# A convolution and SiLU MLP on one core: the first block's taps on square TensorE tiles, and one weight unit rounded in thirds

## The chip, the cores and the metric

The kernel runs on one core of one Trainium2 chip. Its time is the device time of one execution in microseconds (us); the median of several executions is what is compared. The core has five engines with their own instruction queues: TensorE (PE; its weight loads are shown as PEld), VectorE (DVE), ScalarE (ACT), GpSimd (POOL) and SyncE (SP, which here only issues DMAs). Every queue runs in order: an instruction that waits holds up all that stand behind it in its queue.

## The reference

Two stages, 32768 tokens (8 sequences of 4096), 192 channels:

```python
# 1. causal convolution over 7 positions, one softmaxed filter per head (8 heads of 24 channels)
w = softmax(weight)                                  # [8 heads, 7 taps]
out[b, s, h, g] = sum_k w[h, k] * x_pad[b, s + k, h, g]      # x_pad: 6 zeros ahead of each sequence
# 2. an MLP over the tokens, no biases
h = x @ w_in                                         # [32768,192] x [192,2048]
g = h * (1.0 / (1.0 + np.exp(-h)))                   # SiLU
return (g @ w_out).astype(np.float32)                # [32768,2048] x [2048,192]
```

`x` and `weight` are float32; `w_in` and `w_out` come as float64 and are turned into float32 on the chip by integer arithmetic on their two 32-bit words ("rounding" below).

## The kernel before, in words

**Tiling.** The tokens are worked off in 32 blocks of 1024. A block lies as two halves (n = 0, 1) of 512 tokens; its 192 channels lie as three thirds (k = 0, 1, 2) of 64 channels. In tile `xt` partitions 0 to 63 hold the channels of half 0 and partitions 64 to 127 the same channels of half 1, with six tokens of halo ahead of each. The 2048 hidden columns are four units (j = 0 to 3) of 512: a unit of `w_in` is `wr[j]`, a unit of `w_out` is `wo[j]`.

**Blocks 1 to 31** use a saving (Winograd-like) product scheme, `product` (L497) and `out_slot` (L570), whose order is written out by hand in `PLAN`. The change doesn't touch them. **Block 0** is done plainly while the weights are still being rounded, and it is all that the change touches.

**Block 0, in the order of the program.** Almost all instructions are pinned: each engine gets them in program order. `heat` gives TensorE dummy products until data is there. The softmaxed taps reach all partitions by one small product (L365). Then thirds 0 and 1 of the convolution are made on TensorE: `diagonal(k)` lets ScalarE write seven diagonal matrices (the taps of each channel, twice side by side in 128 columns), and `conv_pe(k)` multiplies them with seven shifted views of `xt` (L805, 28 products in all, 64 rows by 128 columns, one per tap, third and half). The two column halves are the same, so the result is already there twice, on partitions 0 to 63 and 64 to 127; ScalarE copies it (`act.copy`, 128x512) into `dups[0]`. Third 2 is convolved on VectorE: `conv(0, 2, i)` is one ScalarE operation for the first tap (L404) and six on VectorE (L409), and `spread` (L421) duplicates it by DMA.

**Rounding.** `round_in(j, k)` rounds one third of unit j (128x256 operations), `round_in(j)` a whole one (128x768). Each has seven or eight VectorE operations, and for units 0 and 1 two of the steps are ScalarE's (`act.sign` and an `act.activation`): VectorE must wait for them, and they stand in ScalarE's queue in program order. Unit 0 is rounded in thirds, units 1 to 3 whole.

**The first products.** `up_plain(0, j)` (L460) makes h of unit j: 24 products of 64 rows by 128 columns into eight PSUM banks (two halves a of the columns, two halves n of the tokens, two 128-column groups e), three thirds k accumulated in each. For unit 0 the thirds are the outer loop, so all eight banks are opened with third 0; for the others each pair of banks is finished before the next. After a bank's last third ScalarE reads it with SiLU. There are only eight PSUM buffers in the pool (`bank()`), handed out in turn, so `up_plain(0, 1)` gets a bank back when ScalarE has read it for unit 0, and two of the banks of unit 0 are those that hold convolved third 1 until it is copied out. ScalarE needs a table load between the functions of the rounding and SiLU.

After that come the other units of `up_plain`, `down_plain` (L599), and block 1. `load` (L128), `halo` (L146) and `load_in` (L218, L223) issue the DMAs for x, its halo and the raw words of `w_in`; the halos of thirds 1 and 2 are issued by GpSimd behind a VectorE memset.

Of the kernel before, what the change touches and what calls it, by code (L numbers as in the profile page):

```python
# [9 lines left out]
F32 = mybir.dt.float32  # L10
# [7 lines left out]
def kernel(  # L18
# [24 lines left out]
    nc = tc.nc  # L43
# [3 lines left out]
    H, K = weight.shape  # L47
    NT = B * S
    DFF = moe_w_in.shape[1]
    P = 128  # L50
    R = 64
    NK = D // R
    grp = D // H
    pad = K - 1
    TB = 512
# [4 lines left out]
    NJ = NM // 2  # L60
# [11 lines left out]
    gpool = ctx.enter_context(tc.tile_pool(name="gp", bufs=2 * NJ))  # L72
    upool = ctx.enter_context(tc.tile_pool(name="up", bufs=13))
# [29 lines left out]
    def pin(ins):  # L103
        return tc.keep_in_program_order(ins)
# [7 lines left out]

    vec, act = Pinned(nc.vector), Pinned(nc.scalar)

    def bank():
        return psum.tile([P, TB], F32, tag="ps", name="ps")

    nats, xts, gs = {}, {}, {}

    def load(b, ks=range(NK)):  # L120
        if b not in nats:
            nats[b] = xpool.tile([P, NK, TB // SQ, SQ], F32, tag="nat", name="nat")
        nat = nats[b]
        for k in ks:
            for i in range(P // SQ):
                c = R * k + SQ * (i % 2)
                queue = nc.scalar if not b and k == 0 and i % 2 == 0 else nc.sync
                ins = queue.dma_start(  # L128
                    out=nat[SQ * i : SQ * i + SQ, k, :, :],
                    in_=x_v[2 * b + i // 2][:, :, c : c + SQ],  # L130
                )
                if not b:
                    pin(ins)
# [10 lines left out]
    def halo(k, queue):  # L144
        pin(
            queue.dma_start(  # L146
                out=xts[0][R:P, k, 0:pad], in_=x0[:, k, :], allow_slow_non_contiguous=True
            )
        )

    halo(0, nc.sync)

    zeros = const.tile([P, P], F32, name="zeros")
    warm = const.tile([P, 1], F32, name="warm")
# [3 lines left out]

    hot = const.tile([KR, 2, R], F32, name="hot")
    wown = const.tile([KR, NK, K], F32, name="wown")  # L160
    one_hot = upool.tile([P, TB], F32, tag="u", name="one_hot")[:, 0:P]
    vec.memset(wown, 0.0)
    vec.memset(one_hot, 0.0)
    pool = Pinned(nc.gpsimd)
# [1 line left out]
    for k in range(NK):  # L166
        rows_k = hot[SQ * k : SQ * k + SQ]
        for sign, base in ((1, 0), (-1, grp - 1)):
# [6 lines left out]
                pattern=[[0, 2], [sign, R]],  # L175
# [1 line left out]
            )  # L177

    for e in range(2):
        half = one_hot[R * e : R * e + R].rearrange("p (a c) -> p a c", a=2)  # L180
        pool.affine_select(
            out=half,
            in_=half,
            compare_op=ALU.not_equal,
            fill=1.0,
            base=0,
            pattern=[[0, 2], [-1, R]],
            channel_multiplier=1,
        )
    pool.memset(xts[0][0:R, :, 0:pad], 0.0)  # L190
# [15 lines left out]
        return raws[key]  # L206


    AS = ["p (k a c) -> p a k c"] + ["p (a k c) -> p a k c"] * (NJ - 1)

    def load_in(j, queue, ks=None):

        if ("i", j) not in raws:
            raw_tile(("i", j))
        raw = raws["i", j].rearrange(AS[j], a=2, k=NK)
        for e in range(2) if ks is None else ():
            for a in range(2):
                queue.dma_start(  # L218
                    out=raw[R * e : R * e + R, a, :, :], in_=in32[:, :, a, 2 * j + e, :]
                )  # L220
        for k in ks or ():
            for e in range(2):
                queue.dma_start(  # L223
                    out=raw[R * e : R * e + R, :, k, :], in_=in32[:, k, :, 2 * j + e, :]
                )
# [53 lines left out]
    def round_in(j, k=None):  # L279

        words = raws["i", j].rearrange(AS[j], a=2, k=NK)
        words = words.rearrange("p a k (c t) -> p a k c t", t=2)
        if k is None:
            rounded(
                wr[j].rearrange("p a k c -> p a (k c)"),
                words.rearrange("p a k c t -> p a (k c) t"),
                j < 2,
            )
        else:
            rounded(wr[j][:, :, k, :], words[:, :, k], j < 2)  # L290
        if k in (None, NK - 1):

            del raws["i", j]
            for e in range(2):
                nc.gpsimd.dma_start(
                    out=ws[j][R * e : R * e + R], in_=wr[j][R - R * e : 2 * R - R * e]
                )
# [8 lines left out]
    def comb(out, u, v, op):  # L306
        nc.gpsimd.tensor_tensor(out, u, v, op=op)
# [13 lines left out]
    def combine_out(j):  # L321


        def a_(u, a):
            return wo[j][:, a, :, HD * u : HD * u + HD]
# [4 lines left out]
        comb(x_[2], a_(0, 1), x_[1], ALU.subtract)  # L330
        comb(a_(1, 0), a_(0, 0), a_(1, 0), ALU.subtract)

    load_in(0, nc.sync, (0,))


    def heat(times):
        for _ in range(times):
            pin(
                nc.tensor.matmul(  # L339
                    idle[:, 0 : 2 * P],  # L340
                    zeros,
                    zeros.unsqueeze(1).to_broadcast([P, 2, P]),
                    start=True,
                    stop=True,
                )
            )
# [5 lines left out]
    heat(4)  # L352
    vec.tensor_reduce(top, wexp, axis=AX.X, op=ALU.max, negate=True)
    act.activation(wexp, wexp, AF.Exp, bias=top, accum_out=total)
    load(0, (1, 2))
    load_in(0, nc.sync, (1, 2))
    vec.tensor_scalar(total, total, scalar1=1e-9, scalar2=None, op0=ALU.add)
    vec.reciprocal(part_, total)
# [11 lines left out]
            stop=True,  # L370
        )
    )
    heat(2)
    vec.tensor_copy(taps.rearrange("p k i -> p (k i)"), by_head)

    tails = {}
# [1 line left out]
    def turn_in(b, k):  # L378
        if k == 0 and b:
            xt = xts[b] = xpool.tile([P, NK, pad + TB], F32, tag="xt", name="xt")  # L380
            if b * TT % S == 0:
                nc.gpsimd.memset(xt[0:R, :, 0:pad], 0.0)
            else:
                nc.gpsimd.tensor_copy(xt[0:R, :, 0:pad], tails.pop(b))
        xt = xts[b]
        pin(
            nc.vector.transpose(
                xt[:, k, pad : pad + TB], nats[b][:, k, :, :].rearrange("p k c -> p (k c)")
            )
        )  # L390
        if k == NK - 1:
            if b:
                nc.sync.dma_start(out=xt[R:P, :, 0:pad], in_=xt[0:R, :, TB : TB + pad])
            if (b + 1) * TT % S:
                tails[b + 1] = xpool.tile([R, NK, pad], F32, tag="tail", name="tail", bufs=2)
                nc.sync.dma_start(out=tails[b + 1], in_=xt[R:P, :, TB : TB + pad])
# [28 lines left out]
    dups, wins = {}, {}  # L425
# [12 lines left out]
        )[i]  # L438
        pin(nc.vector.tensor_tensor(t[:, i, :], u, v, op=ALU.subtract))

    def rows(t, e):
        return t[R * e : R * e + R]

    def g_tile(b, j, a):
        if (b, j, a) not in gs:
            gs[b, j, a] = gpool.tile([P, 2, 2, TB], F32, tag="g", name="g")
# [2 lines left out]
    def up_plain(b, j):  # L449

        d = dups[b]
        outs = [(a, n) for a in range(2) for n in range(2)]
        hs = {(a, n, e): bank() for a, n in outs for e in range(2)}
        order = [(k, o) for k in range(NK) for o in outs]
        if j:
            order = [(k, o) for o in outs for k in range(NK)]
        for k, (a, n) in order:
            for e in range(2):
                pin(
                    nc.tensor.matmul(  # L460
                        hs[a, n, e],
                        rows(wr[j], e)[:, a, k, :],
                        rows(d, e)[:, n, k, :],
                        start=k == 0,
                        stop=k == NK - 1,
                    )
                )
            if k == NK - 1:
                for e in range(2):
                    g = g_tile(b, j, a)  # L470
                    act.activation(g[:, n, e, :], hs[a, n, e], AF.Silu)
# [317 lines left out]

    diag = gpool.tile([P, NK - 1, K, P], F32, tag="g", name="diag")
    dups[0] = xpool.tile([P, 2, NK, TB], F32, tag="dup", name="dup")
    by_pe = {}

    def diagonal(k):
        for i in range(K):
            act.activation(diag[:, k, i, :], one_hot, AF.Copy, scale=taps[:, k, i : i + 1])

    def conv_pe(k):  # L800
        by_pe[k] = [bank() for _ in range(2)]
        for i in range(K):
            for n in range(2):
                pin(
                    nc.tensor.matmul(  # L805
                        by_pe[k][n],
                        rows(diag, n)[:, k, i, :],
                        rows(xts[0], n)[:, k, i : i + TB],
                        start=i == 0,
                        stop=i == K - 1,  # L810
                    )
                )

    turn_in(0, 0)

    vec.memset(xts[0][R:P, 1:NK, 0:pad], 0.0)
    for k in range(1, NK):
        halo(k, nc.gpsimd)
    diagonal(0)
    conv_pe(0)  # L820
    round_in(0, 0)
    diagonal(1)
    turn_in(0, 1)
    conv_pe(1)
    for j in (1, 2):
        load_in(j, nc.sync)
    turn_in(0, 2)
    conv(0, 2, 0)
    for n in range(2):
        act.copy(dups[0][:, n, 0, :], by_pe[0][n])  # L830
    for i in range(1, K):
        conv(0, 2, i)
    spread(0, 2)
    load_in(3, nc.sync)
    round_in(0, 1)
    for n in range(2):
        act.copy(dups[0][:, n, 1, :], by_pe[1][n])
    round_in(0, 2)
    round_in(1)
    for j in range(NJ):  # L840
        up_plain(0, j)
        if j + 2 < NJ:
# [70 lines left out]
```

## Time and profile before

| what | value |
|---|---|
| median of 4 runs (lowest to highest) | 2409.33 us (2409.12 to 2409.73) |
| the profiled execution's own time, and its span | 2410.11 us, 2408.4 us |
| busy share of the span: PE, DVE, ACT | 100%, 86%, 41% |
| TensorE, taps of block 0 (L805) | 7.28 to 19.50 us |
| TensorE, four units of h (L460) | 19.50 to 60.70 us, 10.3 us each |
| TensorE, product with w_out (L599) | 60.70 to 102.05 us |

The span is counted from the first instruction that the profile shows; times "at 7.28 us" are from there. A product of float32 shows as two matmul records. An instruction's line is L111 when it was issued through the helper that pins it. In lines of a timeline the columns are start, time from the first start to the last end, engine, line, operation, output<-inputs, shape and count, and in brackets the idle time of that engine before it with what ended it.

### The profile page before, as it was taken

How to read it: one execution, taken by the hardware profiler on the slowest of the kernel's cores; microseconds unless marked ns; L12 is line 12 of the kernel's file. 1: busy time of each engine (PE TensorE's matmuls, PEld its weight loads, DVE VectorE, ACT ScalarE, POOL GpSimd, SP SyncE). 2: the span in 40 equal slices, each digit the busy share in tenths (PEclk: the TensorE clock that was granted, in tenths of full speed). 3: DMA queues.
4: the chain of work that ended last, by engine and by line, in shares of the span. 5: the costliest groups of instructions: out<-in, count | busy, mean ns of one | idle time of the engine just before them, and what ended most of it. 6: DMA issues, size and time to landing. Idle time of an engine off the chain costs nothing.

```text
span 2408.4 us, 43335 instructions
## 1 busy us (share of the span) xinstructions
PE 2400.7 (100%) x17878; PEld 943.3 (39%) x17878; DVE 2061.7 (86%) x2812; ACT 993.9 (41%) x1873; POOL 70.1 (3%) x99
## 2 busy tenths in 40 slices
PE   9999999999999999999999999999999999999998
PEld 4333443334433344333344333443334433334433
DVE  8789888888888898888988888888889888898876
ACT  4334543334533345433454333453334533345432
POOL 4300000000000000000000000000000000000000
PEclk9999999999999999999999999999999999999999
DMA  7322122221222222222222222122222222222220
GB/s 160 60 44 47 35 36 54 53 41 32 42 47 53 41 41 36 45 54 44 44 38 36 54 50 43 32 39 51 53 41 41 36 45 54 43 43 39 36 40 14
DMA packets 453718, 110.59 MB, mean 46 GB/s; under 512 B 424080, under 2 KB 429200, under 8 KB 453520
## 3 DMA queue, kind: packets, MB, share of 16 engines
q1 hardware_dynamic: 449872, 105.85, 23.9%
q8 instruction: 140, 2.29, 0.4%
q0 software_dynamic: 448, 1.58, 0.3%
q10 hardware_dynamic: 3200, 0.39, 0.1%
q14 instruction: 58, 0.48, 0.1%
HBM read 31.46 MB, written 25.17 MB: 24 GB/s over the span
## 4 chain that ended last, share of the span: by engine, by line
PE 100%; DVE 0%; ACT 0%; issue 0%; ACTq 0%
PE ps L497 49%; PE ps L570 47%; PE ps L599 2%; PE ps L460 2%; PE ps L805 1%; PE ps L339 0%; DVE cmb L111 0%; ACT u L111 0%; DVE osb L111 0%; PE ps L365 0%; ACTq L739 0%; DVE zeros L111 0%; DVE warm L111 0%; ACTq L111 0%
## 5 line engine op out<-in xcount | busy, mean ns | idle before, releaser
L497 PE MATMUL ps<-dup,ws 64*128 64x512 f32 x2480 | 870.0, 589 | 0.0
L570 PE MATMUL ps<-g,wo 128*32 128x512 f32 x2976 | 661.8, 593 | 0.0
L521 DVE TENSOR_TENSOR g<-u,ps 128x512 f32<-128x512 f32 x744 | 486.0, 681 | 119.2 <-PE ps L497 89.8
L497 PE MATMUL ps<-win,wr 64*128 64x512 f32 x1488 | 567.8, 589 | 0.0
L570 PE MATMUL ps<-t,wo 128*32 128x128 f32 (+2 forms) x4528 | 500.6, 446 | 0.0
L518 ACT ACTIVATE g<-g 128x512 f32<-128x512 f32 x744 | 444.6, 631 | 97.3 <-DVE g L521 97.3
L497 PEld LDWEIGHTS ps<-dup,ws 64*128 64x128 f32 x2480 | 363.4, 187 | 291.8 <-issue 277.7
L570 PE MATMUL ps<-t,wx 128*32 128x512 f32 x2976 | 452.8, 592 | 0.0
L409 DVE SCALAR_TENSOR_TENSOR nat<-xt,taps,nat 128x512 f32<-128x512 f32 x564 | 423.5, 751 | 18.3 <-ACT nat L404 3.7
L497 PE MATMUL ps<-dup,wr 64*128 64x512 f32 x992 | 420.1, 596 | 0.0
L512 ACT COPY u<-ps 128x512 f32<-128x512 f32 x496 | 277.7, 588 | 229.3 <-PE ps L497 226.2
L638 ACT COPY cmb<-ps 96x512 f32<-96x512 f32 x30 | 17.4, 581 | 805.3 <-PE ps L570 805.3
L538 DVE TENSOR_TENSOR t<-g 128x1024 f32<-128x1024 f32 x248 | 299.9, 1220 | 27.2 <-PE ps L570 27.2
L538 DVE TENSOR_TENSOR t<-g,t 128x1024 f32<-128x1024 f32 x248 | 303.2, 1223 | 13.6 <-PE ps L570 3.2
L497 PEld LDWEIGHTS ps<-win,wr 64*128 64x128 f32 x1488 | 233.6, 187 | 175.3 <-issue 147.0
L570 PEld LDWEIGHTS ps<-t,wo 128*32 128x32 f32 x4528 | 180.4, 110 | 219.7 <-issue 199.5
L497 PE MATMUL ps<-win,ws 64*128 64x512 f32 x496 | 242.2, 589 | 0.0
L570 PE MATMUL ps<-g,wx 128*32 128x512 f32 x1488 | 234.6, 592 | 0.0
L570 PEld LDWEIGHTS ps<-t,wx 128*32 128x32 f32 x2976 | 121.9, 110 | 278.8 <-issue 269.5
L650 DVE TENSOR_TENSOR cmb<-cmb,ps 96x512 f32<-96x512 f32 x150 | 102.2, 681 | 135.2 <-ACT u L635 133.1
L497 PEld LDWEIGHTS ps<-dup,wr 64*128 64x128 f32 x992 | 160.6, 187 | 128.1 <-issue 114.2
L570 PEld LDWEIGHTS ps<-g,wo 128*32 128x32 f32 x2976 | 168.6, 110 | 98.3 <-issue 98.3
(72 smaller groups left out, 1224.9 us busy)
## 6 DMA issues: line engine op xcount, KB each, us to landing
dup<-nat SPq DMA_DIRECT2D x376, 128.0 KB, 2.3
nat<-in_x_dram SPq DMA_DIRECT2D x382, 64.0 KB, 2.4
out_dram<-osb SPq DMA_DIRECT2D x376, 64.0 KB, 2.0
raw<-in_moe_w_out_dram SPq DMA_DIRECT2D x8, 384.0 KB, 4.0
raw<-in_moe_w_in_dram SPq DMA_DIRECT2D x12, 192.0 KB, 4.5
ws<-wr POOLq DMA_DIRECT2D x8, 192.0 KB, 4.3
raw<-in_moe_w_in_dram SPq DMA_DIRECT2D x6, 128.0 KB, 3.0
xt<-xt SPq DMA_DIRECT2D x31, 4.5 KB, 1.9
```

Of the source, the lines that this page charges most:

```text
L409: nc.vector.scalar_tensor_tensor(out=dst, in0=src, scalar=tap, in1=dst, op0=ALU.mult, op1=ALU.add)
L460: nc.tensor.matmul(hs[a, n, e], rows(wr[j], e)[:, a, k, :], rows(d, e)[:, n, k, :], start=k == 0, stop=k == NK - 1,)
L497: nc.tensor.matmul(bk[b, m, bn], rows(w, half), rows(v, half), start=first, stop=True, skip_group_check=True,)
L512: pin(copy(u, bk[b, m, "1"]))
L518: pin(nc.scalar.activation(g, g, AF.Silu))
L521: pin(nc.vector.tensor_tensor(g, us.pop((b, m, i)), bk[b, m, bn], op=ALU.add))
L538: pin(nc.vector.tensor_tensor(t[i // 2][:, i % 2, :], u, v, op=ALU.subtract))
L570: nc.tensor.matmul(accs[b][at][SQ * q : SQ * q + SQ, to], lhs[:, e, SQ * k : SQ * k + SQ], rhs[:, e, ts(q, TB // 4) if i == 5 else to], st ...
L599: nc.tensor.matmul(acc[k][R * n : R * n + R, :], wo[j][:, a, e, R * k : R * k + R], gs[b, j, a][:, n, e, :], start=j == 0 and a == 0 and e ...
L638: pin(nc.scalar.copy(c[0], acc[0][0:n, :]))
L650: pin(nc.vector.tensor_tensor(out_, u, v, op=ALU.add))
L805: nc.tensor.matmul(by_pe[k][n], rows(diag, n)[:, k, i, :], rows(xts[0], n)[:, k, i : i + TB], start=i == 0, stop=i == K - 1,)
```

## The change

Six edits, all in block 0:

- The diagonal matrices have 64 columns in place of 128, so a tap product writes 64 PSUM partitions. Third k writes partitions 64k to 64k+63 of the bank of its token half: rows come from half n, columns from third k. For each tap the four products (two halves, two thirds) stand next to each other in the queue; all taps of both thirds are one loop (28 products as before).
- The result is there only once, so each is copied twice: `from_pe(k)` issues four 64x512 ScalarE copies per third, eight in all in place of four 128x512.
- Third 1 of `xt` is transposed ahead of the rounding of unit 0's first third, and its four loads are issued ahead of the halo of third 0 and of the first raw words of `w_in`.
- Five dummy products stand behind the tap matrix in place of two.
- Unit 1 of `w_in` is rounded by thirds: 3 x 8 operations of 128x256, with six ScalarE steps in place of two. Its raw words are laid out by thirds for that (`AS`).
- `up_plain(0, 1)` takes thirds as its outer loop, as unit 0 does.

```diff
-    halo(0, nc.sync)
-    one_hot = upool.tile([P, TB], F32, tag="u", name="one_hot")[:, 0:P]
+    one_hot = upool.tile([P, TB], F32, tag="u", name="one_hot")[:, 0:R]
...
-    AS = ["p (k a c) -> p a k c"] + ["p (a k c) -> p a k c"] * (NJ - 1)
+    AS = ["p (k a c) -> p a k c"] * 2 + ["p (a k c) -> p a k c"] * (NJ - 2)
...
+    load(0, (1,))
+    halo(0, nc.sync)
     load_in(0, nc.sync, (0,))
...
-    load(0, (1, 2))
+    load(0, (2,))
     load_in(0, nc.sync, (1, 2))
...
-    heat(2)
+    heat(5)
...
-        if j:
+        if j > 1:
             order = [(k, o) for o in outs for k in range(NK)]
...
-    diag = gpool.tile([P, NK - 1, K, P], F32, tag="g", name="diag")
+    diag = gpool.tile([P, NK - 1, K, R], F32, tag="g", name="diag")
     dups[0] = xpool.tile([P, 2, NK, TB], F32, tag="dup", name="dup")
-    by_pe = {}
-    def diagonal(k): ...
-    def conv_pe(k): ...
+    by_pe = [bank() for _ in range(2)]
     turn_in(0, 0)
     vec.memset(xts[0][R:P, 1:NK, 0:pad], 0.0)
     for k in range(1, NK):
         halo(k, nc.gpsimd)
-    diagonal(0)
-    conv_pe(0)
+    for i in range(K):
+        for k in range(NK - 1):
+            act.activation(diag[:, k, i, :], one_hot, AF.Copy, scale=taps[:, k, i : i + 1])
+    turn_in(0, 1)
+    for i in range(K):
+        for n in range(2):
+            for k in range(NK - 1):
+                pin(
+                    nc.tensor.matmul(
+                        by_pe[n][R * k : R * k + R, :],
+                        rows(diag, n)[:, k, i, :],
+                        rows(xts[0], n)[:, k, i : i + TB],
+                        start=i == 0,
+                        stop=i == K - 1,
+                    )
+                )
     round_in(0, 0)
-    diagonal(1)
-    turn_in(0, 1)
-    conv_pe(1)
     for j in (1, 2):
         load_in(j, nc.sync)
     turn_in(0, 2)
     conv(0, 2, 0)
-    for n in range(2):
-        act.copy(dups[0][:, n, 0, :], by_pe[0][n])
+    def from_pe(k):
+        for n in range(2):
+            for e in range(2):
+                act.copy(rows(dups[0], e)[:, n, k, :], by_pe[n][R * k : R * k + R, :])
+    from_pe(0)
     for i in range(1, K):
         conv(0, 2, i)
     spread(0, 2)
     load_in(3, nc.sync)
     round_in(0, 1)
-    for n in range(2):
-        act.copy(dups[0][:, n, 1, :], by_pe[1][n])
+    from_pe(1)
     round_in(0, 2)
-    round_in(1)
+    for k in range(NK):
+        round_in(1, k)
     for j in range(NJ):
         up_plain(0, j)
```

More of the change, by code (lines that the diff above doesn't have):

```diff
@@ L113, with rows @@
     vec, act = Pinned(nc.vector), Pinned(nc.scalar)
+    def rows(t, e):
+        return t[R * e : R * e + R]
     def bank():
@@ L179 @@
     for e in range(2):
-        half = one_hot[R * e : R * e + R].rearrange("p (a c) -> p a c", a=2)
+        half = rows(one_hot, e)
         pool.affine_select(
@@ L186 @@
             base=0,
-            pattern=[[0, 2], [-1, R]],
+            pattern=[[-1, R]],
             channel_multiplier=1,
@@ L439, in win @@
         pin(nc.vector.tensor_tensor(t[:, i, :], u, v, op=ALU.subtract))
-    def rows(t, e):
-        return t[R * e : R * e + R]
     def g_tile(b, j, a):
@@ L788, in finish @@
             store(2, cols)
-    diag = gpool.tile([P, NK - 1, K, P], F32, tag="g", name="diag")
+    diag = gpool.tile([P, NK - 1, K, R], F32, tag="g", name="diag")
     dups[0] = xpool.tile([P, 2, NK, TB], F32, tag="dup", name="dup")
-    by_pe = {}
-    def diagonal(k):
-        for i in range(K):
+    by_pe = [bank() for _ in range(2)]
+    turn_in(0, 0)
+    vec.memset(xts[0][R:P, 1:NK, 0:pad], 0.0)
+    for k in range(1, NK):
+        halo(k, nc.gpsimd)
+    for i in range(K):
+        for k in range(NK - 1):
             act.activation(diag[:, k, i, :], one_hot, AF.Copy, scale=taps[:, k, i : i + 1])
-    def conv_pe(k):
-        by_pe[k] = [bank() for _ in range(2)]
-        for i in range(K):
-            for n in range(2):
+    turn_in(0, 1)
+    for i in range(K):
+        for n in range(2):
+            for k in range(NK - 1):
                 pin(
                     nc.tensor.matmul(
-                        by_pe[k][n],
+                        by_pe[n][R * k : R * k + R, :],
                         rows(diag, n)[:, k, i, :],
@@ L812, in conv_pe @@
                 )
[L814 to L818, printed above, removed]
-    diagonal(0)
-    conv_pe(0)
     round_in(0, 0)
-    diagonal(1)
-    turn_in(0, 1)
-    conv_pe(1)
     for j in (1, 2):
@@ L835 @@
     round_in(0, 1)
-    for n in range(2):
-        act.copy(dups[0][:, n, 1, :], by_pe[1][n])
+    from_pe(1)
     round_in(0, 2)
-    round_in(1)
+    for k in range(NK):
+        round_in(1, k)
     for j in range(NJ):
```

## The prediction, made before the changed kernel was run

> **What bounds the kernel now.** First the page's busy times and its chain of work that ended last, then that chain in order of time for the first 110 us.
>
> ```profile
> span 2408.4 us, 43335 instructions
> ...
> PE 100%; DVE 0%; ACT 0%; issue 0%; ACTq 0%
> ```
> ```profile
> 1.14 3.78 PE ps L339 x8
> ...
> 7.28 12.22 PE ps L805 x56
> 19.50 41.20 PE ps L460 x192
> 60.70 41.35 PE ps L599 x192
> ```
>
> TensorE works without a gap from 1.14 us to its last product. The change touches nothing behind the first four units of h, so its worth is one number: how much earlier or later TensorE reaches the third unit (j=2), now at 19.34 + 2 x 10.3 = 39.9 us. Everything behind moves by that, unless something else is late there. So the second thing to read is what feeds TensorE before that: VectorE's and ScalarE's timelines.
>
> ```profile
> 7.14 0.61 DVE L111 TENSOR_SCALAR two<-raw 128x256 int32<-128x256 int32 x2 [0.67 <-DMA raw<-in_moe_w_in_dram]
> ...
> 11.10 0.71 DVE L387 STREAM_TRANSPOSE xt<-nat 128x512 f32<-128x512 f32 x1 [0.55 <-DMA nat<-in_x_dram]
> 12.65 4.69 DVE L409 SCALAR_TENSOR_TENSOR nat<-xt,taps,nat 128x512 f32<-128x512 f32 x6 [0.84 <-ACT nat L404]
> 17.26 0.49 DVE L111 TENSOR_SCALAR two<-raw 128x256 int32<-128x256 int32 x2
> ...
> 19.95 0.50 DVE L111 TENSOR_SCALAR two<-raw 128x256 int32<-128x256 int32 x2
> ...
> 22.55 1.02 DVE L111 TENSOR_SCALAR two<-raw 128x768 int32<-128x768 int32 x2
> ...
> 28.25 1.04 DVE L111 TENSOR_SCALAR two<-raw 128x768 int32<-128x768 int32 x2
> ```
> ```profile
> 17.78 0.72 ACT L111 ACTIVATE two<-two 128x256 int32<-128x256 int32 x2 [3.18 <-DVE two L111]
> 19.54 1.07 ACT L111 COPY dup<-ps 128x512 f32<-128x512 f32 x2 [1.03 <-PE ps L805]
> ...
> 23.61 1.58 ACT L111 ACTIVATE two<-two 128x768 int32<-128x768 int32 x2 [2.38 <-DVE two L111]
> 25.20 1.28 ACT L111 ACT_TABLE_LOAD   x1
> 27.26 4.03 ACT L111 ACTIVATE g<-ps 128x512 f32<-128x512 f32 x8 [0.77 <-PE ps L460]
> ```
>
> VectorE is full from 12.65 us on: six convolution steps, then rounding, a third of a unit in 2.65 us (17.26, 19.95, 22.55), unit 1 whole in 5.70. ScalarE's last rounding step is over at 25.19, the table is loaded by 26.48, and the first SiLU starts at 27.26, when TensorE has a bank ready: 0.8 us to spare. That is the tightest place, and the change adds work ahead of it on both engines.
>
> **Part by part.**
>
> *Square tiles.* 28 tap products now take 0.43 us each, two row tiles side by side. Four column tiles already run side by side in the later blocks: four records start within 0.02 us and the next four 0.43 us later.
>
> ```profile
> 600.12 0.61 PE L570 MATMUL ps<-t,wx 128*32 128x512 f32 x3
> 600.13 0.59 PE L570 MATMUL ps<-t,wo 128*32 128x512 f32 x1
> ```
>
> Two rows by two columns is not in this trace; the bounds are 7 x 0.86 = 6.0 us (four at a time) and 28 x 0.43 = 12.0 us (two at a time). I take 6.0, as both directions are seen to run in parallel, and leave 12.0 to a rival.
>
> *When the taps can start.* The fourth product needs the halo of third 1, which until now had until 13.4 us. GpSimd issues it at 6.77 us behind VectorE's memset and it lands 3.1 us later, at 9.9. Memset and issue stay where they are. The five dummy products end between 8.3 and 9.5 us (0.85 us each from 5.24, or half of that from 7.2 us on, where the tap products show the double rate), so they are covered by that wait; if the halo came at once they would cost about 1.1 us against the old start. Taps: 9.9 to 16.1 us with 0.2 us for start and drain, 3.4 us earlier than 19.50. Fourteen 64-column diagonals in place of fourteen of 128 take at most the old 0.30 us each and are there by 9.9; the wait for the halo covers them.
>
> *Copies.* Four in place of two per third: 0.59 + 3 x 0.48 = 2.05 us (a 32x512 copy of the later blocks takes 579 ns, so fewer partitions buy nothing). TensorE could start on h after the first, at 16.8 us, and needs all four for third 0 by 18.2.
>
> The row is 1.07 us for two copies. [...]
>
> *The loads.* SP issues eight loads of x in 4.30 us, 0.54 each. Four of them now pass the first raw words: 4 x 0.44 to 0.54 = 1.7 to 2.2 us, so the first rounding starts at 8.9 to 9.3 in place of 7.14, or less if the transfers overtake; not below 7.14. I take 8.8. Rounding 2.70 us to 11.5, transpose of third 2 (0.71, now behind it alone, its loads having kept their place in the queue and their old arrival at 11.1) to 12.2, ScalarE's first tap 0.84 to 13.05, six steps 4.61: VectorE is free at 17.7 in place of 17.26 (17.2 to 18.2). The earlier transpose of third 1 costs nothing, it falls into the wait for the raw words.
>
> *ScalarE's order.* Behind the first four copies (18.2) stands the pair of rounding steps of third 1 (17.7 + 0.53 = 18.2; 0.72 us), and only behind that the copies of third 1: 18.95 to 21.0. They also free the last two of unit 0's eight banks. So TensorE's last product of third 0 waits until 21.1, and nine products of that row tile follow at 0.86: unit 0 is done at 28.8 in place of 29.6. Of the 3.4 us, 0.8 are left.
>
> *Unit 1 in thirds.* 3 x 2.65 = 7.95 us for 5.70. Its last third starts on VectorE at 17.7 + 2.69 + 2.60 + 2 x 2.65 = 28.3; add 0.2 for waits on ScalarE behind the copies: 28.5. Its ScalarE pair, +0.53 and 0.72: 29.75; table load 1.28: 31.0; only then the first SiLU, 0.62: TensorE gets its first bank for unit 1 at 31.7. It has stood still since 28.8, 2.9 us. Unit 1 with thirds outermost needs all eight banks at once, and they come 0.49 us apart (4.03 us for eight): the last at 35.1. Nine products of 0.86 follow: unit 2 starts at 42.8 in place of 39.9. **Sum: +2.9 us.**
>
> *Behind it.* Rounding of unit 1 ends at 28.5 + 2.65 = 31.15 in place of 28.25, +2.9 too, so VectorE and GpSimd keep their distance to TensorE; unit 2's weights, done at 35.35, had 4.6 us to spare. No new wait there.
>
> **The rivals.**
>
> (1) *Slower, the tiles run two at a time.* Then the taps end at 22.1, the copies at 24.2, and ScalarE's pair for third 1 starts at 24.2 in place of 18.2: all rounding is 6 us later and the sum is +8.9 us: 2418.2. Against it are the four parallel column tiles above. It decides from a tap end of 16.2 us on: each us beyond it is a us on VectorE, so a late halo counts the same way.
>
> (2) *Not slower: ScalarE is free in time.* Were the SiLUs not held up, TensorE could go on at 28.8, but unit 2's weights come 7.1 us (28.25 to 35.35) after unit 1's at 31.15, at 38.3: at best 1.6 us faster, 2407.7. For it: VectorE may get through earlier. Against: with the third-2 loads at their old place it can't be free before 17.26, which leaves +2.4 us, and the order of the SiLUs behind unit 1's last third is fixed.
>
> (3) *The clock falls in the stall.* In the trace it does so at the end: the last product ends at 2401.8, and the clock is halved only at 2406.71, behind a stretch of 3.4 us with nothing on TensorE.
>
> ```profile
> 2399.89:2403.30 3.41, 1.94 (x40) 0.94 (x32) 2.19 (x7) 1.42 (x6) 0.00 (x0) 1.00 0.56 90
> 2403.30:2406.71 3.41, 0.00 (x0) 0.00 (x0) 1.09 (x3) 0.33 (x1) 0.00 (x0) 1.00 0.52 87
> 2406.71:2408.40 1.69, 0.00 (x0) 0.00 (x0) 0.00 (x0) 0.00 (x0) 0.00 (x0) 0.50 0.02 5
> ```
>
> (Columns: stretch, length, busy time of PE, PEld, DVE, ACT and POOL, clock, DMA share, GB/s.) A stall of 2.9 us is under 3.4. Should it fall, the start of the kernel shows the way back: 6 us from the first product to the double rate, up to 3.0 us lost: 2415.2.
>
> [...]
>
> **How the numbers follow.** The profiled execution took 2410.11 (span 2408.4 and 1.7 around it), 0.78 above the median, so: span 2411.3, that execution 2413.0, median 2409.33 + 2.9 = **2412.2 us**. Its own range: VectorE free at 17.2 to 18.2 and the halo up to 1 us later give +2.3 to +4.5, 2411.6 to 2413.9. Chances: this 0.77, rival 1 0.09, a still later halo or other delays of over 4.8 us 0.04, rival 3 0.06, rival 2 0.04. The range reaches from no change to rival 3: 2409.2 to 2415.3. 0.2% is 4.8 us, about what can be told from no change; the forecast lies within it. Slower by over 0.2%: rivals 1 and 3 and the late halo, 0.19; faster by over 0.2% needs weights that VectorE can't deliver: 0.02; within: 0.79.
>
> **What would show it.** Taps on TensorE of about 6 us from 9.9; a wait of the fourth for the halo; eight copies of about 0.5 us; TensorE waiting about 2.9 us for a SiLU at 28.8 to 31.7; the table load near 29.8; unit 2 starting near 42.8; from there no gap. I am wrong if the taps take 12 us, if VectorE reaches the second third at another time than 17.2 to 18.2, or if TensorE waits at a place behind unit 2.

## The result and the profile after

The changed kernel takes 2414.45 us (median of 31 runs, 2413.04 to 2415.75) against 2409.41 us of the kernel before (49 runs, 2409.02 to 2410.13): 1.002 times the time, 95% interval 1.0015 to 1.0025, or 5.0 us more. That is 0.21%, just above the bound of 0.2% that the prediction set, with an interval that holds that bound. That the kernel is slower is not in doubt: its shortest run is 2.9 us longer than the longest of the kernel before. The runs do not lie evenly: six at 2413.04 to 2413.24, twenty-two at 2414.0 to 2414.8, three at 2415.6 to 2415.8. The mean granted clock is 1.000 in the six and 0.998 to 0.999 in the others. Why there are groups is a question of its own below; the profile shown here is from the first group (2413.24 us, span 2411.3 us).

The page of the changed kernel, its first line and the chain of work that ended last by engine:

```profile
span 2411.3 us, 43372 instructions
...
PE 98%; DVE 1%; ACT 0%; SPq 0%; DMA 0%; issue 0%; ACTq 0%; DVEq 0%
```

The chain is no longer TensorE alone: VectorE has 1% of it. The same chain in order of time (start, length, engine, output, line) shows where:

```profile
28.60 0.42 DVE two L111 x2
29.04 0.72 ACT two L111 x2
29.78 1.28 ACT L111
31.08 0.61 ACT g L111
31.73 32.02 PE ps L461 x137
63.74 41.35 PE ps L600 x192
```

Up to 31.7 us VectorE sets the time, at the end with the rounding of unit 1, which goes to and fro between VectorE and ScalarE, and then ScalarE's queue: the last third's pair of steps, the load of the SiLU table, the first SiLU. Only then TensorE gets a bank for unit 1. TensorE's timelines (start, length, engine, line, operation, count, and in brackets the idle time before and its releaser) have the other end of that wait. First the kernel before:

```profile
7.21 12.29 PE L805 MATMUL ps<-xt,diag 64*128 64x512 f32 x56
19.34 41.37 PE L460 MATMUL ps<-dup,wr 64*128 64x512 f32 x192
60.63 5.80 PE L599 MATMUL ps<-g,wo 128*64 128x512 f32 x26
```

Then the changed kernel:

```profile
8.24 1.08 PE L810 MATMUL ps<-xt,diag 64*64 64x512 f32 x6
9.83 6.22 PE L810 MATMUL ps<-xt,diag 64*64 64x512 f32 x50 [0.51 <-DMA xt<-in_x_dram]
15.98 3.75 PE L461 MATMUL ps<-dup,wr 64*128 64x512 f32 x12
20.16 9.19 PE L461 MATMUL ps<-dup,wr 64*128 64x512 f32 x36 [0.43 <-ACT dup L111]
31.73 2.65 PE L461 MATMUL ps<-dup,wr 64*128 64x512 f32 x9 [2.38 <-ACT g L111]
```

The taps are over at 16.05 us, 3.4 us earlier than before, and h is begun 3.4 us earlier (15.98 against 19.34). Of that, 0.3 us are left where unit 0 ends (29.35; before, unit 1 followed without a gap at 29.64), and then TensorE stands still for 2.38 us. By single records unit 2 starts at 42.55 us in place of 39.94 (+2.6), the first product with w_out at 63.67 in place of 60.63 (+3.0). The 0.4 us between the two are one matmul record (0.43 us): the SiLUs free the banks about 0.5 us apart, so the two 64-row tiles of TensorE start unit 1 at 31.73 and at 32.22 us, and they stay a record out of step until the product with w_out, which needs both (the last records ahead of it start at 62.67, 62.73 and 63.16). From there to the last product both kernels take 2341.2 us: nothing is lost or won behind the first four units.

VectorE's and ScalarE's timelines of the changed kernel, at the steps that the prediction had dated:

```profile
8.93 0.50 DVE L111 TENSOR_SCALAR two<-raw 128x256 int32<-128x256 int32 x2 [1.72 <-DMA raw<-in_moe_w_in_dram]
...
13.06 4.69 DVE L413 SCALAR_TENSOR_TENSOR nat<-xt,taps,nat 128x512 f32<-128x512 f32 x6 [0.84 <-ACT nat L408]
17.66 0.49 DVE L111 TENSOR_SCALAR two<-raw 128x256 int32<-128x256 int32 x2
...
28.52 0.49 DVE L111 TENSOR_SCALAR two<-raw 128x256 int32<-128x256 int32 x2
```
```profile
15.31 2.38 ACT L111 COPY dup<-ps 64x512 f32<-64x512 f32 x4 [2.29 <-PE ps L810]
18.19 0.72 ACT L111 ACTIVATE two<-two 128x256 int32<-128x256 int32 x2 [0.49 <-DVE two L111]
18.93 2.37 ACT L111 COPY dup<-ps 64x512 f32<-64x512 f32 x4
...
29.04 0.72 ACT L111 ACTIVATE two<-two 128x256 int32<-128x256 int32 x2 [1.85 <-DVE two L111]
29.78 1.28 ACT L111 ACT_TABLE_LOAD   x1
31.08 4.03 ACT L111 ACTIVATE g<-ps 128x512 f32<-128x512 f32 x8
```

The first rounding starts at 8.93, VectorE is free of the convolution at 17.66, and the last third of unit 1 is begun at 28.52. On ScalarE the table load starts at 29.78, right behind the last pair.

### The profile page after: what moved, and what is told of

It reads as the page before. It is cut to its first block, busy times and chain, and to the rows that moved or that the text cites. A ratio compares the mean times of both kernels' runs of the same rounds, so it can differ in the third digit from the quotient of the medians.

```text
span 2411.3 us, 43372 instructions
## 1 busy us (share of the span) xinstructions
PE 2400.3 (100%) x17884; PEld 946.4 (39%) x17884; DVE 2065.1 (86%) x2828; ACT 996.6 (41%) x1881; POOL 69.2 (3%) x99
## 3 DMA queue, kind: packets, MB, share of 16 engines
q8 instruction: 140, 2.29, 0.4%
## 4 chain that ended last, share of the span: by engine, by line
PE 98%; DVE 1%; ACT 0%; SPq 0%; DMA 0%; issue 0%; ACTq 0%; DVEq 0%
PE ps L498 49%; PE ps L571 46%; PE ps L600 2%; PE ps L461 1%; DVE two L111 0%; DVE nat L413 0%; DMA raw<-in_moe_w_in_dram 0%; ACT two L111 0%; SPq L131 0%; DVE mh L111 0%; DVE cmb L111 0%; DVE wr L111 0%; ACT u L111 0%; ACT L111 0%; DVE osb L111 0%
```

## The experiments

**The two halves of the change, one by one.** The first kernel keeps the square tiles and rounds unit 1 whole again:

```diff
-    AS = ["p (k a c) -> p a k c"] * 2 + ["p (a k c) -> p a k c"] * (NJ - 2)
+    AS = ["p (k a c) -> p a k c"] + ["p (a k c) -> p a k c"] * (NJ - 1)
...
-        if j > 1:
+        if j:
...
-    for k in range(NK):
-        round_in(1, k)
+    round_in(1)
```

> The changed kernel with unit 1 of w_in rounded whole and multiplied pair by pair of banks, as before the change; square tiles, double copies, loads and dummies stay changed. My account (A: SiLU is held up behind unit 1's last third and the table load): ScalarE's pair ends near 26.0 us, the table is loaded by 27.3, TensorE starts unit 1 at 29.2 when its weights are there (23.4 + 5.7) and unit 2 at 39.5: 2409.0, a little faster than before, no stall of over 0.5 us in front of unit 1, and no spread over the runs. Rival B (VectorE, later by 0.4 to 0.8 us since the loads moved, sets the time through the weights of unit 1): the same place, 2409.0 to 2410. Rival C (tiles, copies and loads at the front cost it): still slower, 2412 to 2414.

The second is the kernel before with the opposite of these three edits and nothing else of the change.

> The kernel before with only unit 1 rounded by thirds and multiplied with thirds outermost. A: last third starts on VectorE at 27.75 us, ScalarE's pair ends at 29.0, table at 30.3, first bank at 30.95, TensorE waits 1.3 us and starts unit 2 near 42.1: 2411.5 (+2.1), without the spread, since the stall is short. C: no change, 2409.4.

Against 2409.37 us for the kernel before (33 runs beside them), the square tiles alone took 2409.85 us (ratio 1.0002, interval 0.9993 to 1.0011; all eleven runs within 0.3 us), and the thirds alone 2412.99 us (ratio 1.0015, 1.0006 to 1.0024). So 3.6 of the 5.0 us come with the thirds, and the 0.5 us by which the square tiles alone are longer can't be told from nothing. The time with the square tiles alone lies 0.85 us above what theory A expected and in the range of rival B. TensorE and the chain of waits with the square tiles alone:

```profile
15.72 3.75 PE L461 MATMUL ps<-dup,wr 64*128 64x512 f32 x12
20.09 22.27 PE L461 MATMUL ps<-dup,wr 64*128 64x512 f32 x96 [0.61 <-ACT dup L111]
```
```profile
18.12 0.72 ACT two L111 x2
...
20.66 0.59 ACT dup L111
...
21.29 39.10 PE ps L461 x178
```

There is no pause before unit 1 (29.22 us). What sets the start is no longer the taps but VectorE's rounding, the pair of steps on ScalarE behind it and the copies that stand behind that pair: h is begun 3.6 us earlier, and unit 2 only 0.34 us (39.60 against 39.94).

With the thirds alone, the chain ends as in the changed kernel:

```profile
28.36 0.72 ACT two L111 x2
29.10 1.28 ACT L111
30.40 0.61 ACT g L111
31.05 32.02 PE ps L460 x137
```

The pause is 1.27 us (29.78 to 31.05), and unit 2 starts at 41.88, 1.94 us later than before. The pause is shorter than with both halves because unit 0 ends 0.4 us later and the chain behind the convolution 0.7 us earlier: VectorE begins unit 1's rounding at 22.69 us here and at 23.38 in the changed kernel, where the convolution is over 0.2 us later, behind later raw words, and a rounding step loses 0.4 us waiting for ScalarE behind third 1's copies. That is what the other half adds. The median is 1.5 us above what was expected, and the runs spread, from 2412.08 to 2414.38, though no spread was expected. The profiled run, 2412.41, is 2.3 us above the profiled run of the kernel before (2410.11), near the 2.1 that were expected; what lengthens the five runs from 2413.35 on is in no profile.

**ScalarE out of unit 1's rounding.** In the changed kernel, the two ScalarE steps of each of unit 1's thirds go to VectorE:

```diff
-            rounded(wr[j][:, :, k, :], words[:, :, k], j < 2)
+            rounded(wr[j][:, :, k, :], words[:, :, k], j < 1)
```

> The changed kernel with unit 1's two ScalarE steps per third done by VectorE (one more operation per third, 3.05 us in place of 2.65). A: the table load moves ahead to about 22 us, SiLU follows TensorE, no stall of TensorE over 0.5 us in front of unit 1; weights of the thirds at 26.4, 29.5, 32.5; unit 2's weights at about 39.8 become the limit: 2409.0 to 2409.7. B (VectorE's longer rounding is what holds TensorE): 1.2 us more on VectorE, so slower than the changed kernel or equal, 2414 to 2415.7.

It took 2411.96 us (2410.51 to 2412.41), 2.5 us less than the changed kernel, but not the 2409.7 or less that was expected. The pause before unit 1 is gone (28.69 us). In its place TensorE waits for unit 2's weights, as its timeline says (wr is the rounded weights):

```profile
24.83 14.75 PE L461 MATMUL ps<-dup,wr 64*128 64x512 f32 x66
40.26 20.87 PE L461 MATMUL ps<-dup,wr 64*128 64x512 f32 x96 [0.68 <-DVE wr L111]
```

VectorE, with these steps on it, has unit 2's weights ready at 40.12. It has ten operations per third there in place of eight; two of the thirds take 2.8 us each, but the last takes 4.5 (28.92 to 33.43), where 3.05 were expected. The first product with w_out starts at 61.06, 0.4 us later than before; a further 1.2 us are lost behind it, in the next block; the one gap of TensorE that the profile shows there is 0.1 us (at 122.4), so where the rest arises was not settled. So ScalarE's queue makes the pause, and VectorE stands right behind it as the next limit.

**The table load.** The same change with one SiLU of a 128x1 tile put into ScalarE's free time:

```diff
     round_in(0, 2)
+    act.activation(warm, warm, AF.Silu)
     for k in range(NK):
         round_in(1, k)
```

> The changed kernel with one SiLU of a 128x1 tile on ScalarE behind the rounding of unit 0's last third, so that the table of SiLU is loaded in ScalarE's free time (at about 22 us) and not between unit 1's last rounding step and the first SiLU. The output does not depend on that tile. Theory A (ScalarE's order behind VectorE's rounding makes the pause, pair 0.72 and table load 1.28 us of it): the first SiLU starts at 29.8 in place of 31.08, unit 1 at 30.4 in place of 31.7, pause 1.1 us, unit 2 at 41.3 in place of 42.55: a profile of 2411.9 to 2412.0, 1.25 us less than the profile after; median 2412 to 2413, less spread than the changed kernel. Rival (VectorE's rounding is next at once): unit 1 starts at 30.4 all the same, since its last third is rounded at 29.0 and copied at 29.8, but unit 2 waits for its weights as in the kernel without ScalarE steps on unit 1: they are done at 39.5 to 40.6, ahead of 41.3, so nothing would be lost; a loss of over 0.3 us against theory A speaks for the rival.

2411.74 us, and all eleven runs within 2411.60 to 2411.84. ScalarE's timeline:

```profile
22.10 1.28 ACT L111 ACT_TABLE_LOAD   x1
23.39 0.20 ACT L111 ACTIVATE warm<-warm 128x1 f32<-128x1 f32 x1
...
29.08 0.72 ACT L111 ACTIVATE two<-two 128x256 int32<-128x256 int32 x2 [1.85 <-DVE two L111]
29.82 4.03 ACT L111 ACTIVATE g<-ps 128x512 f32<-128x512 f32 x8
```

The first SiLU starts at 29.82 in place of 31.08, unit 1 at 30.47 behind a pause of 1.10 us, unit 2 at 41.30:

```profile
30.47 14.85 PE L461 MATMUL ps<-dup,wr 64*128 64x512 f32 x65 [1.10 <-ACT g L111]
```

The profiled run (2411.77 us) is 1.47 us below that of the changed kernel, where 1.25 was expected. Unit 2 is 1.25 us earlier, so the table load costs nearly its whole length (1.28) in the changed kernel, and it does so by its place in ScalarE's order. The median fell by 2.7 us, 1.3 more than the shortest runs did (2413.04 to 2411.60): that part is the subject of the next two runs.

**The groups of runs.** To fill the pause, six zero products are added to the sums in unit 0's last two banks (they add zero):

```diff
+            if j == 0 and k == NK - 1 and (a, n) == (1, 1):
+                for _ in range(3):
+                    for e in range(2):
+                        pin(
+                            nc.tensor.matmul(
+                                hs[a, n, e],
+                                rows(zeros, e),
+                                rows(d, e)[:, n, k, :],
+                                start=False,
+                                stop=True,
+                                skip_group_check=True,
+                            )
+                        )
```

> The changed kernel with six products of zero weights put behind unit 0 into its last two banks (they add zero; 6 x 0.43 us = 2.6 us, where TensorE stands still until the first SiLU frees a bank). If the clock falls in the stall in most executions, those of 2414.5 and 2415.7 vanish and all take about 2413.1 at a clock of 1.000. If the spread has another cause, it stays: 2413.0 to 2415.7, median 2414.4.

TensorE's timeline at the pause (L473 are the zero products):

```profile
28.73 3.16 PE L473 MATMUL ps<-dup,zeros 64*128 64x512 f32 x11
31.69 13.56 PE L461 MATMUL ps<-dup,wr 64*128 64x512 f32 x59
```

Unit 2 starts at 42.52 us as before this edit (42.55), and the median is 2413.19 us: nine of eleven runs lie at 2413.10 to 2413.32, at the place of the changed kernel's first group, two at 2413.71 and 2414.06. The work and its order are the same; only TensorE's pause is filled. So the upper groups come from the pause. What happens in it had to be seen in an execution of an upper group, so the changed kernel was run again:

> The changed kernel once more, for a profile of an execution that is not at the short end. The profile after took 2413.24 us with the granted clock at 1.000; most other executions took 2414.3 to 2414.8 and some 2415.7 with the mean clock at .998 to .999. Theory A (the clock falls in or behind TensorE's pause before unit 1): a profile of an execution at about 2414.5 or 2415.7 shows a stretch of less than full clock beginning at 29 to 33 us, 2.4 us or more long, and products of 0.43 us in place of 0.21 each there; from unit 2 on all is as in the profile after. Rival (the spread comes from where the clock first reaches full speed): full clock begins 1 to 2.5 us later than at 6.6 us and no second stretch is seen. If the execution is again at 2413.2 this tells nothing.

This execution took 2414.41 us. The pause before unit 1 is the same, 2.38 us:

```profile
31.66 13.89 PE L461 MATMUL ps<-dup,wr 64*128 64x512 f32 x54 [2.38 <-ACT g L111]
```

Its stretches of 3.41 us around the pause (columns: stretch, length, busy time and count of PE, PEld, DVE, ACT and POOL, the granted clock, DMA share, GB/s):

```profile
28.48:31.90 3.42, 1.04 (x3) 0.24 (x2) 3.27 (x10) 2.89 (x5) 2.84 (x5) 1.00 0.00 0
31.90:35.31 3.41, 3.41 (x9) 2.28 (x10) 3.41 (x6) 3.14 (x7) 2.65 (x5) 0.50 0.96 278
35.31:38.72 3.41, 3.41 (x18) 2.16 (x17) 3.34 (x5) 0.00 (x0) 0.26 (x1) 1.00 0.51 107
```

For one stretch of 3.41 us TensorE runs at half the clock, nine matmul records in place of eighteen, behind a stretch in which it worked for 1.04 of 3.41 us. Unit 2 starts at 43.77, so unit 1 took 12.11 us in place of 10.83: 1.28 us, which is the distance of the two groups (1.35 us between their middles). Half the clock for 3.41 us would be 1.7 us; that the rest hides in the time that unit 1 waits for banks anyway (SiLUs 0.5 us apart) is an estimate. The third group, another 1.2 us on, was in no profile; that it has two such stretches is a guess.

**Can the taps' gain become time?** To the square tiles alone (2409.85 us) two edits are added: ScalarE issues the halos behind its Exp, and the copies of third 1 go ahead of third 1's rounding steps:

```diff
+    for k in range(1, NK):
+        halo(k, nc.scalar)
...
-    for k in range(1, NK):
-        halo(k, nc.gpsimd)
...
     from_pe(0)
+    from_pe(1)
...
     round_in(0, 1)
-    from_pe(1)
```

(The memset that the halos overwrite moves ahead of them.)

> The kernel with unit 1 rounded whole (2409.85 us, taps in square tiles kept), and two more edits: ScalarE issues the halos of thirds 1 and 2 right behind its Exp, so that the taps do not wait for them, and the copies of third 1 stand ahead of third 1's rounding steps on ScalarE. It asks whether the 1.6 us that the taps gain at the front of TensorE can become time at all. Theory A (VectorE's rounding decides when unit 1 may start, whatever TensorE gains before): taps from 8.3 us, unit 0 over at about 27.6 in place of 29.2, but unit 1 still waits for its rounded weights until 29.1 to 29.3: 2409.8, within 0.3 us of the kernel without the two edits; and with a pause of TensorE of 1.6 us before unit 1 some executions 1 us longer. Rival (TensorE's front is on the path): unit 1 starts at 27.6 to 28 and unit 2 1.2 to 1.6 us earlier than 39.60: 2408.2 to 2408.6.

2410.63 us (2409.76 to 2411.35), so not faster; the profiled run (2409.82) is level with the kernel without the two edits, and the median is 0.8 us above it. TensorE's timeline:

```profile
7.37 6.42 PE L810 MATMUL ps<-xt,diag 64*64 64x512 f32 x56
14.42 5.32 PE L464 MATMUL ps<-dup,wr 64*128 64x512 f32 x16 [0.62 <-ACT dup L111]
20.78 24.71 PE L464 MATMUL ps<-dup,wr 64*128 64x512 f32 x106 [1.04 <-DVE wr L111]
```

The taps run without a gap from 7.37 and h is begun at 14.42, nearly 5 us ahead of the kernel before, but TensorE then waits for VectorE's second third (20.78), and unit 1 starts at 29.45. Its weights are ready no earlier than 29.1, as VectorE's timeline has it:

```profile
28.16 0.96 DVE L111 SCALAR_TENSOR_TENSOR wr<-mh,two 128x768 f32<-128x768 f32 x1
```

So the start is VectorE's: a further gain on TensorE only lengthens its wait. In this execution the clock is halved in the 3.41 us behind the stretch with that wait, which delays unit 0 but unit 1 by 0.3 us at most (29.45 against 29.12):

```profile
17.66:21.07 3.41, 2.29 (x8) 0.64 (x7) 3.23 (x11) 1.61 (x4) 0.00 (x0) 1.00 1.15 206
21.07:24.48 3.41, 3.41 (x10) 1.40 (x10) 3.26 (x10) 0.81 (x3) 0.76 (x2) 0.50 0.90 224
```

Some executions were expected to be 1 us longer, and five of the eleven are (2411.17 to 2411.35). But their mean granted clock is 0.999 to 1.000 and that of the shortest two 0.999, and the profile of a short one has the fall; so what lengthens them stays open.

**The kernel before, one zero product less.**

```diff
-    heat(2)
+    heat(1)
```

> The kernel before with one zero product fewer behind the product that spreads the taps: heat(1) in place of heat(2). The output does not depend on it. In the kernel before TensorE has no gap from 1.14 us to its end, and the first tap waits only for these products, ending at 7.24 us; the diagonal is there at 6.1. Theory A (in the kernel before TensorE is the bound from its first product on, with 0.8 us to spare before the first SiLU): up to 0.4 us (one product at the double rate) less, 2409.0. Rival (the first SiLU, and so VectorE's and ScalarE's rounding, is the bound as in the changed kernel): 2409.4, no change.

2409.22 us (2409.04 to 2411.23) against 2409.54 us (27 runs): ratio 1.0000, interval 0.9991 to 1.0009. The shortest runs of both are the same (2409.04 and 2409.01), so no gain is shown and neither theory confirmed. The one run at 2411.23 was the profiled one: there the record of the full clock begins at 10.5 us, not at 7.1 as in the profile of the kernel before, with ten matmul records in the 3.41 us ahead of it and eighteen in those behind (the columns are those of the stretches above):

```profile
7.11:10.52 3.41, 3.41 (x10) 1.49 (x8) 3.21 (x9) 3.41 (x12) 1.20 (x2) 1.00 0.78 127
10.52:13.93 3.41, 3.41 (x18) 1.64 (x16) 1.97 (x3) 0.74 (x2) 0.00 (x0) 1.00 0.72 219
```

Its first products with w_in start at 20.59 in place of 19.34. In this execution the late full clock thus moved the time of this kernel, in which nothing hides it. No kernel of these is measurably faster than the one before.

## Why the prediction was right or wrong

The forecast was 2412.2 us in a range of 2409.2 to 2415.3, with a change within 0.2% as likeliest (0.79). The measured 2414.45 lies in the range, 2.2 us above the forecast; at 0.21% above the kernel before it is by a hair in the class "slower by over 0.2%", which had 0.19. The account of what makes the kernel slower was right; two things behind it were not, the step to the median and the clock. By its steps:

- *Four tiles at a time.* Right: of the 28 products (56 records) three (6 records) run from 8.24 us, the fourth waits for the halo, and the other 50 records take from 9.83 to 16.05 us; forecast 9.9 to 16.1. Rival 1 is out.
- *The loads, VectorE and the halo.* Right: first rounding 8.93 (8.8), VectorE free at 17.66 (17.7), halo landed at 9.83 (9.9).
- *Copies.* Mis-sized: 2.38 us for four, not 2.05; they follow each other 0.6 us apart. Third 0's did not decide: the pair of third 1 had its input only at 18.19. The copies of third 1 ended at 21.30 (21.0), and VectorE, idle for 0.53 us ahead of 21.78, lost 0.43 us by them, where 0.2 was allowed.
- *ScalarE's order and unit 1.* Right in mechanism: pair from 29.04, table load at 29.78 (29.75), first SiLU at 31.08 (31.0), unit 1 at 31.7 (31.7); VectorE began the last third at 28.52 (28.5), in part by luck: the 0.2 us too little for the wait were made up by thirds of 2.57 us in place of 2.65. The table load was shown to cost its 1.28 us by moving it, the thirds as a whole to carry 3.6 us by taking them alone. The pause is 2.38 us, not 2.9, since unit 0 ended at 29.35 and not 28.8; that shortens the pause, not the time.
- *Sum +2.9.* Unit 2 was reached 2.6 us later, the products with w_out 3.0 (the row tiles out of step, which the sum did not have), and the profiled run is 2413.24 against the forecast 2413.0 for it. "No new wait there": right, from w_out on the rest takes as long as before.
- *From the profiled execution to the median: wrong, 0.9 us.* The step took 0.78 us off, because the profile of before was that much above the median. The changed kernel's shortest runs are 2413.04, as long as the profiled one within 0.2 us. Taking the square tiles alone likewise gives runs within 0.3 us, where the kernel before spreads over 1.1. That the spread of the kernel before is the arrival of the full clock, which in the changed one hides in the wait for the halo and behind VectorE, fits these runs and the one with a late clock; it was not tried by itself.
- *Rival 3, the clock in the pause: underrated in chance, overrated in price.* It was given 0.06 and up to 3.0 us. By the groups it happens in most runs (25 of 31 lie in the upper ones, all at a mean clock under 1.000), and it costs 1.28 us in the one profile that shows it. The step that failed is the threshold: "a stall of 2.9 us is under 3.4". The fall at the end of the kernel, behind 3.4 us of nothing, was taken as the least that it needs, when it was only one instance. A pause of 2.38 us was enough.

Ahead of the end of a kernel, the profiles above show the clock halved in two places, each time for 3.41 us: 31.90 to 35.31 us in the changed kernel's second profile, 21.07 to 24.48 with the earlier unit 0. In the 3.41 us before, TensorE was at work for 1.04 and for 2.29 us, so 3.41 us wholly without work are not needed.

The step to the median and the clock make up the 2.2 us between forecast and median: 0.9 to the shortest group (2413.1), 1.3 from there to the median. Of the rival "not slower", the part that VectorE is next in line was right: without ScalarE's steps on unit 1, and with TensorE's front earlier still, VectorE held the time at no less than it is with the square tiles alone (shortest runs 2410.51 and 2409.76 against 2409.67).

The copies out of PSUM grew from 1.07 us for two to 2.38 for four, and with the square tiles alone third 1's copies do stand in the chain (0.59 us at 20.66); but drawn ahead of the rounding steps they gave no time, since VectorE's weights for unit 1 came no earlier (29.12 us, against 29.07 with the square tiles alone). Giving VectorE a part of the copies would load the engine that is next in line here; that was not tried.

## What to carry to other kernels

A faster stage is worth what the next feeder lets through: here 3.4 us won on TensorE met VectorE's rounding, which had no slack, so before speeding up a stage, read from the timelines when its successor's inputs are ready. When a step is cut into pieces for an earlier start, look at what stands behind the last piece in its engine's queue: a table load and the first SiLU waited for it, and one tiny SiLU placed earlier took 1.25 us of it away. A pause on TensorE should be priced with the clock as well, and by a look at several executions, since by the groups of runs the same pause cost 1.3 us more in most of them and nothing in others.

## What was not expected of the hardware

- The same pause of 2.38 us leaves the clock alone in one execution and halves it for 3.41 us in another. In the changed kernel's first profile the record of the full clock runs from 6.60 to 2409.58 us, in the second the clock is halved from 31.90 to 35.31. Counted in stretches of 3.41 us, the length of that fall, back from the fall in the one and on from 6.60 us in the other, the pause lies differently: in one stretch (28.48 to 31.90, 1.04 us of work) where the clock fell, and over two (27.08 to 30.49 and 30.49 to 33.90, 2.27 and 2.17 us of work) where it did not; that this makes the difference was not shown. The two stretches of the first profile:

```profile
27.08:30.49 3.41, 2.27 (x10) 0.73 (x6) 3.23 (x10) 1.55 (x4) 1.38 (x3) 1.00 0.17 42
30.49:33.90 3.41, 2.17 (x9) 1.39 (x10) 3.38 (x6) 3.40 (x7) 3.41 (x6) 1.00 0.43 127
```

- How much work keeps the clock up stays open: at 2.17 of 3.41 us it stayed up here, at 2.29 it fell in the kernel with the earlier unit 0, and at 2.31 it stayed up with the table load early (28.73 to 32.14 us). Busy time of TensorE as the profile models it does not by itself give a limit for these cases.
- A copy of 64x512 out of PSUM takes as long as one of 128x512 (0.58 and 0.59 us), and the four here follow each other 0.6 us apart, where the two of 128x512 before overlapped (1.07 us for both). Why the smaller ones do not overlap was not looked into.
